# Third chunk's decays by scans from the open banks, key masks ahead of exponentials, early fades on GpSimd

## The chip, the cores and the metric

The kernel runs on one core of a Trainium2 chip. The metric is the time of one execution on the device, in microseconds (us). The kernel before takes 615.42 us, the median of three runs (615.21 to 615.60).

## What is computed

A state-space layer is followed by a weighted mixture of four small networks. Sequences of 768 tokens (4 of them, 8 heads of 32 channels, 16 states) go through the first in chunks. The decay from token j to token i is the exponential of a difference of summed logarithms, which is also the product of the decays in between:

```python
log_a = np.log(np.clip(a, 1e-06, 1.0))
...
    cum = np.cumsum(la, axis=-1)
    L = np.exp(cum[:, :, :, None] - cum[:, :, None, :])
    L = L * causal
    CB = np.einsum('bhin,bhjn->bhij', Cc, Bc)
    M = CB * L
    y_intra = np.einsum('bhij,bhjd->bhid', M, xc)
    y_inter = np.einsum('bhin,bhnd->bhid', Cc, state) * decay_to_i[:, :, :, None]
...
    state = decay_full[:, :, None, None] * state + np.sum(Bx, axis=2)
```

Its output is turned into 3072 tokens of 256 features, and each token gets the sum over four experts:

```python
p = domain_probs / (domain_probs.sum(-1, keepdims=True) + 1e-09)
for e in range(E):
    h = np.maximum(x @ w1[e], 0.0)
    out += p[:, e:e + 1] * (h @ w2[e])
```

Everything is float32.

## The kernel before

**Tiling.** Tokens come in 24 chunks of 128, numbered so that chunks 0 to 3 are the first of each of the four sequences, 4 to 7 the second, and so on. Four blocks of three pairs of chunks go through the experts one after the other. Expert weights come in pieces of 256 hidden features; sums of pieces (fast matrix multiplication with fewer products) are made on VectorE or GpSimd (`difference`, recorded at L1077), and from the second block on read back from DRAM. The products of the experts all have one line, L1017; the copies, sums and gates around them are L1026, L1031, L1044, L1052, L1175 and L1317.

**One chunk of the state-space part** needs four things. `mask` (L495, ScalarE) makes the key mask `ctm`: the chunk's C, once with the odd and once with the even heads set to zero. `score` (L502, TensorE) multiplies it with B into four PSUM banks of two chunks each. The decays L lie in `MT` or `LT`, and VectorE multiplies scores into them (L685 in the opening; L931 for one chunk at a time, L940 for two). A `fade`, recorded at L885 or L545, scales B by the decay to the chunk's end and puts it beside them. `inner` (L551, TensorE) makes outputs and the chunk's own state. From chunk 4 on, L963 adds what the earlier state gives; it reads `cts` (L915, GpSimd), which is the key mask scaled by decays.

**Decays are made in two ways.** Most chunks take exponentials: `sum_logs` turns logarithms of all decays into running sums by matrix products, the sums are stored to DRAM (`cum_d`), `load_decays` (L463) reads one chunk's back, spread over all partitions (`ab`, 512 KB), and `decay` (L526, ScalarE) makes eight exponentials. A causal cut then sets the upper half to zero, on VectorE (L532) where `CUT` says so and on GpSimd (L536) elsewhere. The chunks in `SCANS`, and chunks 0 and 1, take scans instead: `scan` (L519, VectorE) runs along a row of raw decays, multiplies by the decay and adds the identity, so that each partition's product starts at its own token, and no cut is wanted. For chunks 0 and 1 `spread` (L663) puts the raw decays on all partitions by a matrix product into banks, and the scan reads these; chunk 4 reads raw decays from DRAM (`acut_d`).

**The order.** The opening, up to L795, is written out by hand: instructions run in the order of the code on each engine. Behind it, `Plan` takes the rest: every piece of work is added with a duration for each engine that may do it, TensorE's order is given (`line`), and `Plan.run` simulates all engines, starting from the times given in `begin`, and picks on each engine the ready piece with the earliest due time. The order that comes out is then issued. `now` is the planner's clock at the end of the opening; `plan.taken` tells it which buffers are in use and from when their data can be had. A GpSimd piece that shares a port with VectorE is made to wait for the last VectorE instruction with two operands that stands ahead of it in the planned order (L1607).

**DMAs** of the loads and stores are issued by SP, in order. A load whose data is not yet stored holds up SP and all loads behind it.

Just behind the opening, TensorE's order is: second halves of two first-layer products (L726), two more first-layer products, the scores of chunks 2 and 3, four second-layer products (which need the first two second-layer pieces, `W[4]` and `W[5]`), the outputs of chunks 2 and 3, three more products, the scores of chunks 4 and 5, and so on:

```python
for seq, _ in plain[:EARLY]:
    line.extend(seq)
scores([2, 3])
...
line.extend(own_[:OWN])
outputs([2, 3])
```

Of the kernel before, what the change touches and what calls it, by code (L numbers as in the profile page):

```python
# [35 lines left out]
SCORED, OWN, LEAD, LEFT = 7, 4, 5, 3  # L36
SCANS = 4,
FILLED, EARLY, FADE = 3, 4, "DVE"
CUT = {(c, 0): "DVE" for c in range(2, 6)}
HORIZON, OPENING, LOADED = 26.0, 80.0, -0.5  # L40
ORDERS = (0, 1, 2, 3), (3, 1, 2, 0), (0, 1, 2, 3), (3, 1, 2, 0)
PAIRS_AT = ((1, 18, "s0"), (2, 1, "o0"), (2, 1, "s1"), (2, 24, "s2"), (3, 1, "o12")), (
    (1, 1, "s0"), (1, 24, "s1"), (2, 1, "o01"), (2, 24, "s2"), (3, 1, "o2"))
# [27 lines left out]
class Plan:  # L71
# [109 lines left out]
    def run(self, line, at, begin):  # L181
# [16 lines left out]
        stuck = 0  # L198
        self.stall, self.port, self.bus = [], 0.0, begin["SP"] + 4
        self.lanes = [begin["SP"] + .5 * i for i in range(LANES)]  # L200
# [160 lines left out]
def kernel(  # L361
# [25 lines left out]
    HALF = P // 2  # L387
    SPREAD = 2
    blocks = []
# [166 lines left out]
    def keep_state(c, A, y):  # L556
# [8 lines left out]
    aq0 = homes["V"][-1][:, 0].rearrange("p (t s) -> p t s", t=NT)  # L565
    aq1 = homes["V"][-2][:, 0].rearrange("p (t s) -> p t s", t=NT)
    a_q = [aq0, aq1]

# [10 lines left out]
    nc.scalar.dma_start(  # L579
        out=aq1.rearrange("(q r) t s -> q r (t s)", q=NQ)[:, 0], in_=a_rows[:, 1])  # L580
    nc.scalar.preload_act_table_set("natural_log_exp_and_others")
# [45 lines left out]
    nc.vector.reciprocal(total_p, total_p)  # L627
    clip(nc.vector, aq1.rearrange("p t s -> p (t s)"), own)
    nc.vector.memset(aq1[:, :, 0:1], 0.0)

# [28 lines left out]

    def spread(c, banks, half=0):  # L660
        for q, b in enumerate(banks):
            k = slice(32 * q, 32 * q + 32)
            nc.tensor.matmul(  # L663
                out=b[:, NT * P * half:NT * P * (half + 1)], lhsT=one[k].to_broadcast([32, P]),
                rhs=a_q[c][k].rearrange("p t s -> p (t s)"),
                start=True, stop=True, tile_position=(32 * q, 0))
# [89 lines left out]
    for fb in range(2, 4):  # L756
        load_w1(fb, homes["W"][fb])
    for fb in range(2):
        load_w2(fb, homes["W"][4 + fb])
    for c in range(2, 4):  # L760
        load_decays(c, homes["ab"][c - 2])
    for fb in range(2, 4):
        load_w2(fb, homes["W"][4 + fb])
# [4 lines left out]
    fade(0, MT[0], xb[0], LT[0])  # L768
    idle(four[2], 3)
    score([1], ctm[1:], xb[1:2], four, (2, 3, 1, 0))  # L770
    scan_quarters(LT[1], seven, 1, 0)
# [8 lines left out]
    for fb in range(2):  # L780
        first_half(seven[2 + fb], homes["W"][fb], yT0, 0)
    mask(2, ctm[0], xb[2])
    fade(1, MT[1], xb[1], LT[1])
# [17 lines left out]
    B512, B256 = {"DVE": D512, "POOL": 1.3}, {"DVE": D256, "POOL": .72}  # L801
    now = 12.5

# [28 lines left out]
    for c, i in ((2, 2), (3, 3)):  # L832
        st[c]["xb"] = plan.taken("xb", i, now)
    st[2]["ctm"] = plan.taken("ctm", 0, now)
    halves = [plan.taken("bank", homes["bank"].index(seven[2 + fb])) for fb in range(2)]
    for b in seven[:2]:
        plan.homes["bank"][homes["bank"].index(b)].free = now + .6
    for c in range(2, 4):
        st[c]["ab"] = plan.taken("ab", c - 2, now - 2.0 + 1.5 * c)
    for c in range(2):  # L840
        st[c]["A"] = plan.taken("A", c, now)
    g0 = gates[0, 0] = plan.taken("gate", 0, now)
    LTv = [plan.taken("V", 2 * (c % 2) + i, now) for c in SCANS for i in range(2)]
    neg = plan.taken("neg", 0, now - 3.0)
    cd, pd, ad = (plan.taken("dram", i, now) for i in range(3))

    def fetch(c):
        s = st[c]
        if "xb" not in s:
            s["xb"] = value("xb")  # L850
            dma(lambda e: load_tokens(c, s["xb"].t), 2 * len(turned(c)) - 1, 320,
                part=[s["xb"]])
        if c >= NSEQ:
            s["ah"] = value("ah")
            dma(lambda e: load_heads(c, s["ah"].t), len(turned(c)), 64,
                part=[s["ah"]], reads=[cd])
        if "ab" not in s:
            s["ab"] = value("ab")
            URGENT[len(plan.all)] = SOON if c < 6 else 0.0
            dma(lambda e: load_decays(c, s["ab"].t), 1, 512, part=[s["ab"]],  # L860
                reads=[ad if c in SCANS else cd])

    def decays(c):
# [6 lines left out]
        made, early = {}, c < blocks[0].n  # L870
        for h in range(0, NH, NQ) if c in SCANS else ():
            made[h] = dve(1.15, lambda e, h=h: scan(
                LT0[:, j], s["ab"].t[:, h * P:h * P + NQ * P], place(c, h) * P),
# [465 lines left out]
    def plain_first(fb):  # L1339
        w, y = weights["S", fb, 1], yT[0, 0]  # L1340
        if fb < len(halves):
            b = halves[fb]
            seq = [plan.add({"PE": .44}, lambda e: first_half(b.t, w.t, y.t, 1), reads=[w, y], writes=[b])]
            return seq, gated(b, gate_of(0, fb), 0)
# [111 lines left out]
    for fb in range(4):  # L1456
        loaded[fb, 1] = plan.taken("W", fb, now + (0.0 if fb < 2 else .5))
        loaded[fb, 2] = plan.taken("W", 4 + fb, now + (0.0 if fb < 2 else 1.5 + .75 * fb))
    for (fb, l), v in loaded.items():
# [135 lines left out]
    for i, w in enumerate(leave_last(len(blocks) - 1, O, LAST)):  # L1595
        behind.insert(len(behind) - TAILS[i], w)
    line.extend(behind)

    done = plan.run(line, now, {"PE": now, "DVE": now - 1.2, "ACT": now + .7, "POOL": now - 1.8,
                                "SP": now + LOADED})  # L1600
# [55 lines left out]
```

## Time and profile before

| what | us |
|---|---|
| median of three runs | 615.42 |
| the profiled execution, its own time | 614.88 |
| its span, first to last instruction | 613.2 |
| TensorE (PE) busy | 602.8 |
| VectorE (DVE) busy | 488.9 |
| ScalarE (ACT) busy | 299.2 |
| GpSimd (POOL) busy | 155.6 |

The profile is of one execution; times in it count from its first instruction. PE is TensorE's products, PEld its weight loads, which overlap them; PEq, ACTq and SPq are the engines' sequencers. A row of the timeline gives start and length in us, engine, line, operation, tiles (written <- read), shape and count; what stands in brackets is the engine's idle time before it and what ended it. Ends of matrix products are modelled, so that a stretch of products is better measured from its first start to the start of what follows. A row of the waits gives who waited for what: us in total, how often, and the longest.

Other rows of the opening that are used later (start, length, engine, what):

```profile
4.78 2.43 DVE L519 TENSOR_TENSOR_SCAN LT<-bank,ident 128x256 f32<-128x256 f32 x4 [0.39 <-PE bank L663]
5.39 0.94 SPq L460 DMA_DIRECT2D xb<-in_xbc_dram  x2
7.78 2.42 DVE L519 TENSOR_TENSOR_SCAN LT<-bank,ident 128x256 f32<-128x256 f32 x4
9.25 0.80 PE L502 MATMUL bank<-ctm,xb 32*128 32x256 f32 x8
9.98 0.70 PE L551 MATMUL bank<-MT,xb 128*32 128x144 f32 x16
10.49 0.98 SPq L483 DMA_DIRECT2D w<-in_w_dram  x2
11.86 0.82 SPq L463 DMA_DIRECT2D ab<-cum_d  x2
13.67 0.51 ACT L793 COPY v<-bank 128x128 f32<-128x128 f32 x2 [1.35 <-PE bank L551]
14.96 0.21 DVE L994 STREAM_TRANSPOSE S<-A 128x32 f32<-128x32 f32 x1 [3.50 <-ACT A L561]
```

### The profile page before, as it was taken

To read this page: it belongs to the slowest core of one execution; us is meant where nothing else is said; L and a number is where in the kernel's file an instruction comes from. 1 tells how busy PE (TensorE), PEld (TensorE's weight loads), DVE (VectorE), ACT (ScalarE), POOL (GpSimd) and SP (SyncE) were. 2 spreads that over 40 slices of the span, in tenths; PEclk is the share of its full clock that TensorE was granted. 3 is DMA by queue.
4 is the path that set the end of the run, shared out by engine and by line. 5 is a ranking of instruction groups with operands and counts; after the bars stand their busy time and mean duration, and the time that the engine had idled before them with its cause. 6 is when DMAs were issued, how large, how long until landed. Compare 5 with 4: busy or idle time off the path is not lost.

```text
span 613.2 us, 10055 instructions
## 1 busy us (share of the span) xinstructions
PE 602.8 (98%) x3377; PEld 513.5 (84%) x3377; DVE 488.9 (80%) x845; ACT 299.2 (49%) x707; POOL 155.6 (25%) x196
## 2 busy tenths in 40 slices
PE   8899999999999999999999999999999999999996
PEld 5677878888888888888888888888888888888885
DVE  5789898989999895877988988396785989575784
ACT  5766555389442327958252333834444142434441
POOL 5645654647443000777200100200000000000000
PEclk9999999999999999999999999999999999999999
DMA  7956668887733329792422325952242332964001
GB/s 224 318 160 211 218 207 279 291 290 259 271 105 100 84 43 359 257 294 107 154 88 79 115 43 151 317 194 91 70 137 66 106 73 40 356 202 130 1 0 53
DMA packets 88688, 100.30 MB, mean 164 GB/s; under 512 B 26932, under 2 KB 54204, under 8 KB 88636
## 3 DMA queue, kind: packets, MB, share of 16 engines
q1 hardware_dynamic: 88484, 99.60, 51.0%
q8 instruction: 27, 0.44, 0.3%
q14 instruction: 25, 0.20, 0.1%
q10 hardware_dynamic: 152, 0.05, 0.0%
HBM read 79.45 MB, written 20.17 MB: 162 GB/s over the span
## 4 chain that ended last, share of the span: by engine, by line
PE 91%; DVE 3%; DMA 2%; ACT 2%; POOL 1%; issue 1%; SPq 0%; DVEq 0%; ACTq 0%
PE bank L1017 87%; PE bank L551 2%; PE bank L502 2%; DMA ab<-cum_d 1%; DVE v L1044 1%; DVE v L1052 1%; PE bank L963 1%; ACT A L561 1%; ACT MT L526 1%; DVE bank L1175 1%; DMA cum_d<-cum 0%; DMA pr<-in_probs_dram 0%; POOL w L1077 0%; ACT v L978 0%; DVE v L1368 0%
## 5 line engine op out<-in xcount | busy, mean ns | idle before, releaser
L1017 PE MATMUL bank<-v,w 128*128 128x256 f32 x1592 | 377.7, 380 | 0.7 <-DVE v L1052 0.3
L1017 PEld LDWEIGHTS bank<-v,w 128*128 128x128 f32 x1592 | 301.0, 190 | 45.8 <-issue 3.3
L1017 PE MATMUL bank<-Y,w 128*128 128x256 f32 x692 | 177.5, 381 | 0.8 <-ACT LT L978 0.4
L1017 PEld LDWEIGHTS bank<-Y,w 128*128 128x128 f32 x692 | 130.2, 190 | 22.2 <-issue 1.5
L1317 ACT COPY v<-bank 128x512 f32<-128x512 f32 x109 | 63.9, 586 | 173.1 <-PE bank L1017 170.8
L1044 DVE TENSOR_TENSOR v<-v,v 128x512 f32<-128x512 f32 x185 | 136.1, 751 | 2.4 <-ACT v L1026 0.9
L1052 DVE SCALAR_TENSOR_TENSOR v<-bank,gate 128x512 f32<-128x512 f32 x144 | 98.8, 688 | 34.4 <-PE bank L1017 31.1
L1077 POOL TENSOR_TENSOR w<-w,w 128x512 f32<-128x512 f32 (+1 forms) x74 | 82.0, 1118 | 48.5 <-DVE v L1044 12.5
L1175 DVE TENSOR_TENSOR bank<-bank,v 128x512 f32<-128x512 f32 x85 | 58.1, 696 | 34.0 <-PE bank L1017 22.9
L1026 ACT COPY v<-bank 128x512 f32<-128x512 f32 x101 | 59.0, 587 | 51.3 <-PE bank L1017 40.2
L1031 ACT COPY bank<-v 128x512 f32<-128x512 f32 (+1 forms) x127 | 73.5, 590 | 11.5 <-DVE v L1052 6.0
L1017 PE MATMUL bank<-LT,w 128*128 128x256 f32 x276 | 69.8, 379 | 0.0
L1017 PEld LDWEIGHTS bank<-LT,w 128*128 128x128 f32 x276 | 52.4, 190 | 7.1
L526 ACT ACTIVATE MT<-ab,neg 128x128 f32<-128x128 f32 x168 | 53.2, 391 | 6.5 <-DMA ab<-cum_d 6.3
L536 POOL TENSOR_SCALAR_AFFINE_SELECT MT<-MT 128x512 f32<-128x512 f32 x39 | 26.9, 693 | 80.5 <-ACT MT L526 57.5
L940 DVE TENSOR_TENSOR MT<-bank,MT 128x512 f32<-128x512 f32 x40 | 25.3, 682 | 1.6 <-PE bank L502 1.4
L1044 DVE TENSOR_TENSOR v<-bank,v 128x512 f32<-128x512 f32 x27 | 18.6, 688 | 9.0 <-PE bank L1017 7.5
L1368 DVE TENSOR_TENSOR v<-v,v 128x256 f32<-128x256 f32 x55 | 21.4, 423 | 1.1 <-ACT v L1317 0.7
L1317 ACT COPY LT<-bank 128x512 f32<-128x512 f32 x12 | 7.0, 586 | 28.0 <-PE bank L1017 25.2
L1052 DVE SCALAR_TENSOR_TENSOR v<-v,gate 128x512 f32<-128x512 f32 x27 | 20.3, 753 | 0.4
L1052 DVE SCALAR_TENSOR_TENSOR LT<-bank,gate 128x512 f32<-128x512 f32 x18 | 12.4, 688 | 9.4 <-PE bank L1017 7.8
L502 PE MATMUL bank<-ctm,xb 32*128 32x256 f32 x192 | 14.4, 404 | 2.1 <-ACT ctm L495 2.1
(125 smaller groups left out, 306.4 us busy)
## 6 DMA issues: line engine op xcount, KB each, us to landing
w<-w_d SPq DMA_DIRECT2D x128, 256.0 KB
w<-in_w_dram SPq DMA_DIRECT2D x72, 256.0 KB
w_d<-w SPq DMA_DIRECT2D x64, 256.0 KB
ab<-cum_d SPq DMA_DIRECT2D x21, 512.0 KB
gate<-p_d SPq DMA_DIRECT2D x15, 384.0 KB
xb<-in_xbc_dram SPq DMA_DIRECT2D x17, 192.0 KB
xb<-in_xbc_dram SPq DMA_DIRECT2D x7, 320.0 KB
out_dram<-v SPq DMA_DIRECT2D x128, 16.0 KB
```

The costliest lines, as they stand in the source:

```text
L502: nc.tensor.matmul(out=views[r][:, j], lhsT=xb[j][k, OBT:OBT + P], rhs=ctm[j][k].rearrange("p t s -> p (t s)"), start=(j == 0), stop=True, ...
L526: nc.scalar.activation(out=MT[:, place(c, h), 0:P], in_=ab[:, h * P:h * P + P], func=AF.Exp, bias=neg[:, h % NT, NQ * real(c) + h // NT:NQ ...
L536: nc.gpsimd.affine_select(out=MT[:, h:h + n, 0:P], in_=MT[:, h:h + n, 0:P], compare_op=ALU.is_ge, fill=0.0, base=0, pattern=[[0, n], [1, P ...
L940: nc.vector.tensor_mul(to, g, to)
L1017: nc.tensor.matmul(out=o, lhsT=w[:, j], rhs=x if half is None else x[:, j], start=(start and j == 0), stop=(j == 1), skip_group_check=True)
L1026: act(.5, lambda e: nc.scalar.copy(out=flat(v), in_=bank.t), reads=[bank], writes=[v])
L1031: act(.54 if to - lo > FB else .32, lambda e: nc.scalar.copy(out=bank.t[:, lo:to], in_=flat(v)[:, lo:to]), reads=[v], writes=[bank])
L1044: plan.add(engines, lambda e: (on(e).tensor_add if sign > 0 else on(e).tensor_sub)(flat(v), whole(x), whole(y)), reads=[x, y], writes=[v], ...
L1052: dve(D512, lambda e: nc.vector.scalar_tensor_tensor(out=h.t, in0=whole(x).rearrange("p (j m) -> p j m", j=JJ), scalar=0.0, in1=g.t[:, 2 * ...
L1077: (on(e).tensor_add if sign > 0 else on(e).tensor_sub)(out, x, y)
L1175: dve(D512, lambda e: (nc.vector.tensor_add if sign > 0 else nc.vector.tensor_sub)(to.t, bank.t, whole(x)), reads=[x, bank], writes=[to])
L1317: act(.5, lambda e: nc.scalar.copy(out=flat(v), in_=bank.t), reads=[bank], writes=[v], hold=HOLD)
```

## The change

Chunk 2 (the third) joins the chunks that scan, and does it as chunks 0 and 1 do: its raw decays are loaded with chunk 1's (`a_q` has three parts), clipped with them, spread by four more matrix products into the free halves of the four banks that hold chunk 0's, ahead of chunk 1's scores, and scanned from there by VectorE in the planned part. Its exponentials, its causal cut and its load of stored sums go away. Its score products, and chunk 3's, are made one chunk at a time (L931) instead of two at once (L940).

The key masks of chunks 2 and 3 are both made in the opening, in buffers of their own; before, only chunk 2's was, and chunk 3's stood in the planned part.

The fades of chunks 2 to 5 go from VectorE to GpSimd (`FADE`).

SP issues chunk 3's stored sums first and all four second-layer pieces behind them; before, two of these stood ahead of the sums of chunks 2 and 3.

The planner's numbers change with it: its clock at the end of the opening, the starts of the engines, the time at which loads land, the duration of the second halves (1.02 instead of 0.44), and the place of one pair's scores (behind 20 products instead of 18).

```diff
-SCANS = 4,
-FILLED, EARLY, FADE = 3, 4, "DVE"
+SCANS = 2, 4
+FILLED, EARLY, FADE = 3, 4, "POOL"
-HORIZON, OPENING, LOADED = 26.0, 80.0, -0.5
+HORIZON, OPENING, LOADED = 26.0, 80.0, 0.0
-PAIRS_AT = ((1, 18, "s0"), (2, 1, "o0"), (2, 1, "s1"), (2, 24, "s2"), (3, 1, "o12")), (
+PAIRS_AT = ((1, 20, "s0"), (2, 1, "o0"), (2, 1, "s1"), (2, 24, "s2"), (3, 1, "o12")), (
...
-        self.stall, self.port, self.bus = [], 0.0, begin["SP"] + 4
+        self.stall, self.port, self.bus = [], 0.0, begin["SP"] + 3
...
-    SPREAD = 2
+    SPREAD = 3
...
-    aq1 = homes["V"][-2][:, 0].rearrange("p (t s) -> p t s", t=NT)
-    a_q = [aq0, aq1]
+    aq1 = homes["V"][-2].rearrange("p c (t s) -> p c t s", t=NT)
+    a_q = [aq0, aq1[:, 0], aq1[:, 1]]
...
-        out=aq1.rearrange("(q r) t s -> q r (t s)", q=NQ)[:, 0], in_=a_rows[:, 1])
+        out=aq1.rearrange("(q r) c t s -> q r c (t s)", q=NQ)[:, 0], in_=a_rows[:, 1:SPREAD])
...
-    clip(nc.vector, aq1.rearrange("p t s -> p (t s)"), own)
-    nc.vector.memset(aq1[:, :, 0:1], 0.0)
+    clip(nc.vector, aq1.rearrange("p c t s -> p (c t s)"), own)
+    nc.vector.memset(aq1[:, :, :, 0:1], 0.0)
...
-    for fb in range(2):
-        load_w2(fb, homes["W"][4 + fb])
-    for c in range(2, 4):
-        load_decays(c, homes["ab"][c - 2])
-    for fb in range(2, 4):
+    load_decays(3, homes["ab"][0])
+    for fb in range(4):
         load_w2(fb, homes["W"][4 + fb])
...
     idle(four[2], 3)
+    spread(2, four, 1, (2, 3, 1, 0))
     score([1], ctm[1:], xb[1:2], four, (2, 3, 1, 0))
...
-    mask(2, ctm[0], xb[2])
+    for c in range(2, 4):
+        mask(c, ctm[c], xb[c])
...
-    now = 12.5
+    now = 14.0
...
-    st[2]["ctm"] = plan.taken("ctm", 0, now)
+        st[c]["ctm"] = plan.taken("ctm", c, now)
+    st[2]["a"] = [plan.taken("bank", homes["bank"].index(b), now - 2.7) for b in four]
...
-    for c in range(2, 4):
-        st[c]["ab"] = plan.taken("ab", c - 2, now - 2.0 + 1.5 * c)
+    st[3]["ab"] = plan.taken("ab", 0, now + 1.5)
...
-    LTv = [plan.taken("V", 2 * (c % 2) + i, now) for c in SCANS for i in range(2)]
+    LTv = [plan.taken("V", i, now - 2.7) for i in range(2)]
...
         for h in range(0, NH, NQ) if c in SCANS else ():
+            if c < SPREAD:
+                made[h] = dve(1.2, lambda e, h=h: scan_quarters(
+                    LT0[:, j], [b.t for b in s["a"]], 1 - j, h // NQ),
+                    reads=s["a"][h // 2:h // 2 + 2], part=[LTv[h // NQ]])
+                continue
...
-            seq = [plan.add({"PE": .44}, lambda e: first_half(b.t, w.t, y.t, 1), reads=[w, y], writes=[b])]
+            seq = [plan.add({"PE": 1.02}, lambda e: first_half(b.t, w.t, y.t, 1), reads=[w, y], writes=[b])]
...
-        loaded[fb, 2] = plan.taken("W", 4 + fb, now + (0.0 if fb < 2 else 1.5 + .75 * fb))
+        loaded[fb, 2] = plan.taken("W", 4 + fb, now + 1.5 + .75 * fb)
...
-    done = plan.run(line, now, {"PE": now, "DVE": now - 1.2, "ACT": now + .7, "POOL": now - 1.8,
+    done = plan.run(line, now, {"PE": now, "DVE": now - 2.6, "ACT": now + .9, "POOL": now - 1.6,
                                 "SP": now + LOADED})
```

## The prediction

> **What bounds the kernel now.** I read the page first, then the busy time by stretches, then TensorE's waits, then the chain of waits and the timeline of the opening. The page and two of the stretches:
>
> ```profile
> PE 602.8 (98%) x3377; PEld 513.5 (84%) x3377; DVE 488.9 (80%) x845; ACT 299.2 (49%) x707; POOL 155.6 (25%) x196
> 20.00:25.00 5.00, 2.91 (x22) 2.21 (x19) 4.42 (x9) 4.85 (x17) 2.46 (x4) 1.00 1.03 349
> 300.00:400.00 100.00, 100.00 (x570) 86.27 (x572) 78.91 (x143) 43.81 (x96) 6.85 (x9) 1.00 0.43 132
> ```
>
> The columns of a stretch are its length, then PE, PEld, DVE, ACT and POOL, then the granted clock, the DMA share and GB/s. TensorE is busy for all of 300 to 400 at clock 1.00, and for 2.91 of 5 us from 20 to 25. So time can be won where TensorE stands idle, which is in the opening, and lost anywhere. TensorE's waits, longest first:
>
> ```profile
> PE bank L502 <- ACT ctm L495: 2.1, 1, 2.1
> PE bank L688 <- PEq L1648: 0.8, 1, 0.8
> PE bank L1433 <- DVE v L1368: 0.7, 1, 0.7
> PE bank L1017 <- ACT LT L978: 0.4, 1, 0.4
> ```
>
> The longest is one stop of 2.1 us: the scores of chunk 3 (L502) wait for its key mask (L495, on ScalarE). The chain of waits shows why that mask is late (start, length, what):
>
> ```profile
> 9.10 2.69 DMA cum_d<-cum
> ...
> 12.25 7.99 DMA ab<-cum_d
> ...
> 20.32 1.28 ACT MT L526 x4
> 21.60 0.58 ACT ctm L495 x2
> 22.18 1.01 ACT MT L526 x4
> ```
>
> The mask hangs on nothing late. It stands in ScalarE's queue behind exponentials that wait for decays out of DRAM. The timeline has the same place on the engines (start, length, engine, line, operation):
>
> ```profile
> 11.63 0.69 ACT L495 ACTIVATE ctm<-xb,tmask 128x128 f32<-128x128 f32 x2
> 18.90 2.70 ACT L526 ACTIVATE MT<-ab,neg 128x128 f32<-128x128 f32 x8 [3.97 <-DMA ab<-cum_d]
> 19.43 0.71 PE L502 MATMUL bank<-ctm,xb 32*128 32x256 f32 x8
> 22.23 0.71 PE L502 MATMUL bank<-ctm,xb 32*128 32x256 f32 x8 [2.09 <-ACT ctm L495]
> 22.88 3.72 PE L1017 MATMUL bank<-v,w 128*128 128x256 f32 x16
> 26.53 1.73 PE L551 MATMUL bank<-MT,xb 128*32 128x144 f32 x32
> 30.98 1.15 PE L502 MATMUL bank<-ctm,xb 32*128 32x256 f32 x16
> 32.05 3.80 PE L1017 MATMUL bank<-v,w 128*128 128x256 f32 x16
> ```
>
> **Part 1, the key mask of chunk 3 goes ahead of the exponentials.** Before, from the first score matmul (19.43) to the next product (22.88) are 3.45 us. The same sixteen score matmuls without a stop, for chunks 4 and 5, take from 30.98 to 32.05, which is 1.07. If both masks are there, TensorE gains 3.45 - 1.07 = 2.38 us. The mask needs chunk 3's tokens; their load is issued at 5.39 to 5.90, and the store issued behind it at 9.10 on the same queue has landed by 11.79. The added mask costs ScalarE 0.69 at about 12.3, inside the 1.35 us that it stands idle before the copies at 13.67. Were the tokens late, L793 would be late by as much, and TensorE with it. I take -2.38 (bounds: -2.38 to 0).
>
> **Part 2, chunk 2's decays by four scans from the open banks.** TensorE gets four more spread matmuls (eight passes) ahead of chunk 1's scores. Eight score passes of the same shape start at 9.25 and the next group at 9.98, so 0.73 with a change of operand; sixteen passes of chunks 4 and 5 take 1.07, so 0.54 for eight. Everything in this stretch of TensorE stands back to back, so I take +0.55 (bounds: 0, if the step hides in the 0.55 us of load idle ahead of 9.25, to +0.75). The clip of chunk 1's decays, now with chunk 2's beside them, goes from 256 to 512 columns, 0.25 us more (the row for 256) ahead of the first scan at 4.78, where VectorE stood idle 0.39: nothing; the longer memset stands where VectorE waits for the first load.
>
> The four scans take 2.42 us (the four scans from banks at 7.78). VectorE has 1.44 busy of 5 us from 10 to 15 and 1.88 from 15 to 20, and stands idle 3.50 us ahead of 14.96 for chunk 1's state, so they cost nothing. If that cover were gone, the gates of the first products would be late by up to 2.4 us, and they are wanted only at 22.88. The scans hold four banks until about 14.5, or 17.6 if they queue behind chunk 1's state; the next scores want them at about 20.
>
> Eight exponentials (2.70 us of ScalarE), one half-chunk causal cut on VectorE (0.69), one on GpSimd (0.63 to 0.72) and one load of 512 KB go away. SP now issues chunk 3's decays ahead of all four second-layer loads. That load still waits for the store landing at 11.79, and the four loads stand behind it in SP's queue: the first two were issued at 10.49 and 11.00 and now come after about 12.2. By size, chunk 3's decays have 1 MB less ahead of them: landing 20.24 goes to about 17 (1 MB at the 285 to 310 GB/s of these stretches is 3.4 us). The first two second-layer blocks land near 18 and 19, and are wanted at 21. Chunk 3's exponentials then run from 17 to about 19.7.
>
> **Part 3, fades on GpSimd.** Eight fades leave VectorE (six at 0.30 and two at 0.21 on average, so 2.2 us) and go to GpSimd, where the same shape takes 0.29. GpSimd's busy time from 20 to 35 is 2.46 + 4.66 + 3.76 = 10.9 of 15 us; four of the eight fall there, the first four mostly earlier. Each has to wait for VectorE's last two-operand instruction in the planned order, and the cuts, weight sums and state scales behind it wait with it. I count nothing on the path (bounds: -0.5 to +3; the rivals price the upper end).
>
> Fades and VectorE do hold each other up: VectorE's fade takes 213 ns at least and 746 at most, the long one beside a GpSimd cut that ran 1.55 us where others ran 0.63. The score products that the fades now run beside read a bank and one tile (0.41 to 0.42 in L685 and L931, in company of GpSimd or not), so I count no loss for them; rival (a) has the other case.
>
> **Part 4, the outputs of chunks 2 and 3.** TensorE reaches them at 26.53 + 0.55 - 2.38 = 24.7. Their last operands: scores end at about 21.0, and eight products of 256 columns instead of four of 512 take 8 x 0.41 = 3.3 us (L685, L931), against 4 x 0.69 = 2.7. They end at about 24.1 if the cuts and fades of chunk 3 (exponentials to 19.7, cut 0.7, fade 0.3) are done by 20.7. Before, from 26.53 to the next product at 28.19 took 1.66, while chunks 4 and 5 took from 36.38 to 37.49, 1.11. So between -0.55 and, with one gate of 0.69 in between, +0.7; I take -0.3.
>
> **Part 5, the new calibration.** The planner's start of 14.0 and its 1.02 for the first halves move the whole order, and one pair's scores go two products later. From 40 to 66 TensorE waits 1.6 us in all for VectorE and ScalarE; later it waits 0.4 for L978 and 0.9 in the tail. VectorE has about 2 us less to do by 33, and the weights are free to land 1.7 us earlier. Against that, another order may make other short waits. I take 0 (bounds: -1.0 to +2.0).
>
> **The sum:** -2.38 + 0.55 - 0.3 = -2.1 us. Against the profiled execution, 614.88 with a span of 613.2 and 1.7 around it, this is 612.8. That execution lies 0.54 below the median of 615.42, so the median comes to 613.3.
>
> **The rivals.** (a) The fades hold VectorE up. If each of the eight stops a VectorE sum for its whole 0.29 us, that is 2.3 us, and VectorE is the next bound: from 50 to 60 it is busy 10.00 of 10 us, and the chain runs through it from 46 to 63. The gain of 2.1 is then gone: 615.6 at the worst, 615.0 if two in three of them do. For it speaks the row of 746 ns above; against it that VectorE stood waiting for TensorE at 42.12 (1.19 us), so by then it had caught up. The Trainium skill, "SBUF — State Buffer", section "Who interferes with whom", has a rule for this: a VectorE instruction with two SBUF inputs and a GpSimd instruction that reads SBUF contend for one port pair, and the later one is blocked outright. The trace agrees as far as that one row goes; by the rule the sum would come to about no change, by the other rows it stays at -2.1.
>
> (b) Slower: GpSimd becomes the bound. The scaled queries of chunks 4 and 5 (L915, 1.41 us) ran from 32.09 to 33.5, after a wait of 1.24 for VectorE's fade. TensorE wanted them at 35.79 (L963), and wants them at about 33.7 after the change. Four fades ahead of them, each 0.29 and a wait of 0.5 to 0.8 for its turn (GpSimd's waits for VectorE here are 0.3 to 1.2), push them back by 3.2 to 4.4 us, the cut that went gives 0.7 back: done at 36.0 to 37.2. By the upper end the outputs of chunks 4 and 5 start at 37.3 instead of 35.8, and all behind them 1.5 late: 616.9. It decides once the scaled queries come over 2.2 us later than now. Against it: GpSimd's weight sums can go to VectorE, which the planner decides by due times.
>
> (c) The masks do not come ahead in fact: chunk 3's tokens land after 13.6. ScalarE then stands before L793, and the 0.55 is paid besides: 616.0. Against it speaks the landing at 11.79 above.
>
> **How the numbers follow.** What a measurement of this kernel can tell from no change is about 0.2%, here 1.23 us. The forecast has a chance of 0.56 (its own range 611.8 to 614.2), (a) 0.15, (b) 0.23, (c) 0.06. Faster by over 0.2%: the forecast, 0.56. Slower by over 0.2%, that is over 616.65: nearly all of (b) and a little of (c), 0.24. Between: 0.20. The range runs from 611.8, where the calibration gives another 1.5 us, to 617.2, where GpSimd's lateness is carried on; that leaves out about 0.1 at each end.
>
> **What would show it.** In the profile after: no wait of L502 for L495; ScalarE's second mask before 14 us; sixteen score matmuls of chunks 2 and 3 in one go at about 20; four scans from banks between 11 and 18; the outputs of chunks 2 and 3 starting at 24.5 to 25; L963 at about 33.7 without a wait for GpSimd. The prediction is wrong if a wait of over 1 us stands at one of the last two, or if the waits from 40 to 130 add up to over 1 us more than now.

## The result, and the profile after

The changed kernel takes 611.65 us (median of 6, 610.93 to 612.22) against 615.32 us (median of 6, 614.11 to 617.87): ratio 0.9938, interval 0.9917 to 0.9959. A second series gave 611.32 against 615.78, ratio 0.9937 (0.9917 to 0.9957). The forecast was 613.3, with a range from 611.8. The sign and the place were right, the forecast gain was too small.

In the new listing the lines of the planned part that are used here are 4 later: L1017 is L1021, L931 is L935, L963 is L967, L1077 is L1081. The page, two stretches (length, then PE, PEld, DVE, ACT, POOL, clock, DMA share, GB/s) and TensorE's waits after the change:

```profile
PE 603.0 (99%) x3385; PEld 514.7 (84%) x3385; DVE 488.3 (80%) x843; ACT 296.6 (49%) x699; POOL 153.9 (25%) x204
20.00:25.00 5.00, 5.00 (x41) 3.92 (x44) 3.59 (x10) 1.90 (x7) 4.92 (x9) 1.00 0.92 289
300.00:400.00 100.00, 100.00 (x578) 86.02 (x578) 78.86 (x142) 43.79 (x96) 7.41 (x10) 1.00 0.42 130
PE bank L688 <- PEq L1652: 0.8, 1, 0.8
PE bank L1437 <- DVE v L1372: 0.7, 1, 0.7
PE bank L688 <- DVE LT L519: 0.5, 1, 0.5
PE bank L1021 <- ACT LT L982: 0.4, 1, 0.4
PE bank L502 <- ACT A L561: 0.4, 1, 0.4
```

TensorE is busy for all of 20 to 25, and the stop of 2.1 us is gone. The last row shown is new. Rows of the chain of waits and of the timeline of the opening, in the same columns as before:

```profile
9.25 3.35 DMA cum_d<-cum
...
12.66 4.16 DMA ab<-cum_d
```

```profile
11.56 2.42 DVE L519 TENSOR_TENSOR_SCAN LT<-bank,ident 128x256 f32<-128x256 f32 x4
12.20 1.28 ACT L495 ACTIVATE ctm<-xb,tmask 128x128 f32<-128x128 f32 x4
16.91 2.45 ACT L526 ACTIVATE MT<-ab,neg 128x128 f32<-128x128 f32 x8 [1.38 <-DMA ab<-cum_d]
20.03 1.15 PE L502 MATMUL bank<-ctm,xb 32*128 32x256 f32 x16
21.11 3.72 PE L1021 MATMUL bank<-v,w 128*128 128x256 f32 x16
24.76 1.19 PE L551 MATMUL bank<-MT,xb 128*32 128x144 f32 x32
25.88 2.86 PE L1021 MATMUL bank<-v,w 128*128 128x256 f32 x12
27.50 0.31 ACT L917 ACTIVATE dec<-ah 128x128 f32<-128x128 f32 x1 [0.32 <-DMA ah<-cum_d]
27.71 0.63 ACT L982 COPY v<-bank 128x256 f32<-128x256 f32 x2
28.37 1.50 ACT L561 COPY A<-bank 32x32 f32<-32x32 f32 x8
29.16 1.90 PE L502 MATMUL bank<-ctm,xb 32*128 32x256 f32 x16 [0.42 <-ACT A L561]
30.99 3.80 PE L1021 MATMUL bank<-v,w 128*128 128x256 f32 x16
```

Both masks stand at 12.20, the scans run from banks at 11.56, chunk 3's exponentials start at 16.91, and sixteen score matmuls run in one go at 20.03. At 29.16 TensorE comes to the scores of chunks 4 and 5 too early. They want banks that ScalarE still empties (L561), and ScalarE was held up by a decay (L917) that waited for a DMA behind the late store (3.35 us instead of 2.69). In the second profile of the changed kernel the loads came earlier, and the stop is hardly there:

```profile
26.07 2.86 PE L1021 MATMUL bank<-v,w 128*128 128x256 f32 x12
...
28.86 1.22 PE L502 MATMUL bank<-ctm,xb 32*128 32x256 f32 x16
...
30.00 2.29 PE L1021 MATMUL bank<-v,w 128*128 128x256 f32 x9
```

The starts of the same TensorE groups, read off the timelines, in us (difference to before in brackets):

| group | before | after | after, second profile |
|---|---|---|---|
| second halves, L726 | 13.99 | 14.60 (+0.61) | 14.79 (+0.80) |
| scores of chunks 2 and 3 | 19.43 | 20.03 (+0.60) | 20.22 (+0.79) |
| product behind them | 22.88 | 21.11 (-1.77) | 21.30 (-1.58) |
| product behind outputs of 2 and 3 | 28.19 | 25.88 (-2.31) | 26.07 (-2.12) |
| product behind scores of 4 and 5 | 32.05 | 30.99 (-1.06) | 30.00 (-2.05) |
| product behind outputs of 4 and 5 | 37.49 | 36.43 (-1.06) | 35.44 (-2.05) |
| product behind the scores at 80 to 83 | 84.37 | 82.06 (-2.31) | 81.16 (-3.21) |
| last but one turn of the output | 604.17 | 601.85 (-2.32) | 600.95 (-3.22) |

From 84 us on nothing moves any more. But 2.3 to 3.2 us in the profiles stand against 3.7 to 4.5 in the medians: one more thing differs between executions.

### The profile page after: what moved, and what is told of

Read it like the earlier page. It is cut to its first block, busy times and chain, and to the rows that moved or that the text cites. A ratio compares the mean times of both kernels' runs of the same rounds, so it can differ in the third digit from the quotient of the medians.

```text
span 610.5 us, 10066 instructions
## 1 busy us (share of the span) xinstructions
PE 603.0 (99%) x3385; PEld 514.7 (84%) x3385; DVE 488.3 (80%) x843; ACT 296.6 (49%) x699; POOL 153.9 (25%) x204
## 4 chain that ended last, share of the span: by engine, by line
PE 93%; DMA 2%; ACT 2%; DVE 1%; issue 0%; POOL 0%; SPq 0%; ACTq 0%; DVEq 0%; POOLq 0%
PE bank L1021 88%; PE bank L502 2%; PE bank L551 2%; DMA ah<-cum_d 1%; ACT A L561 1%; PE bank L967 1%; DMA ab<-cum_d 1%; PE bank L688 1%; DMA cum_d<-cum 1%; POOL w L1081 0%; ACT v L982 0%; DVE bank L1179 0%; ACT MT L526 0%; DVE LT L519 0%; DVE v L1372 0%
## 5 line engine op out<-in xcount | busy, mean ns | idle before, releaser
L1021 PE MATMUL bank<-v,w 128*128 128x256 f32 x1640 | 385.3, 380 | 0.0
L1021 PEld LDWEIGHTS bank<-v,w 128*128 128x128 f32 x1640 | 310.4, 190 | 45.3 <-issue 2.1
L1021 PE MATMUL bank<-Y,w 128*128 128x256 f32 x692 | 177.5, 381 | 0.8 <-ACT LT L982 0.4
L1021 PEld LDWEIGHTS bank<-Y,w 128*128 128x128 f32 x692 | 130.2, 190 | 22.2 <-issue 1.5
L1321 ACT COPY v<-bank 128x512 f32<-128x512 f32 x106 | 62.1, 585 | 173.9 <-PE bank L1021 172.9
L1048 DVE TENSOR_TENSOR v<-v,v 128x512 f32<-128x512 f32 x174 | 130.2, 760 | 1.3
L1081 POOL TENSOR_TENSOR w<-w,w 128x512 f32<-128x512 f32 (+1 forms) x74 | 80.2, 1094 | 55.1 <-DVE v L1048 15.1
L1030 ACT COPY v<-bank 128x512 f32<-128x512 f32 x99 | 57.9, 586 | 49.2 <-PE bank L1021 42.7
L1179 DVE TENSOR_TENSOR bank<-bank,v 128x512 f32<-128x512 f32 x79 | 53.7, 694 | 33.4 <-PE bank L1021 23.7
L1035 ACT COPY bank<-v 128x512 f32<-128x512 f32 x126 | 72.8, 594 | 10.6 <-DVE v L1056 7.3
L1021 PE MATMUL bank<-LT,w 128*128 128x256 f32 x228 | 58.0, 379 | 0.0
L1021 PEld LDWEIGHTS bank<-LT,w 128*128 128x128 f32 x228 | 43.2, 190 | 6.1 <-issue 0.3
L1372 DVE TENSOR_TENSOR v<-v,v 128x256 f32<-128x256 f32 x45 | 17.8, 417 | 1.1 <-ACT v L1321 0.7
L1048 DVE TENSOR_TENSOR v<-v,LT 128x512 f32<-128x512 f32 x25 | 16.9, 683 | 0.3
```

The source lines that it names most:

```text
L1021: nc.tensor.matmul(out=o, lhsT=w[:, j], rhs=x if half is None else x[:, j], start=(start and j == 0), stop=(j == 1), skip_group_check=True)
L1030: act(.5, lambda e: nc.scalar.copy(out=flat(v), in_=bank.t), reads=[bank], writes=[v])
L1035: act(.54 if to - lo > FB else .32, lambda e: nc.scalar.copy(out=bank.t[:, lo:to], in_=flat(v)[:, lo:to]), reads=[v], writes=[bank])
L1048: plan.add(engines, lambda e: (on(e).tensor_add if sign > 0 else on(e).tensor_sub)(flat(v), whole(x), whole(y)), reads=[x, y], writes=[v], ...
L1081: (on(e).tensor_add if sign > 0 else on(e).tensor_sub)(out, x, y)
L1179: dve(D512, lambda e: (nc.vector.tensor_add if sign > 0 else nc.vector.tensor_sub)(to.t, bank.t, whole(x)), reads=[x, bank], writes=[to])
```

## The experiments

Where the text gives short waits between products, it is the time from one start to the next beyond the usual 0.217 us, summed over a stretch wherever it is more than 0.12 us. By this count the kernel before has 1.65 us from 36 to 66 and 0.28 from 66 to 130, and the changed kernel has 0.40 and 0.28 in both of its profiles.

**Chunk 3's mask alone.** From the kernel before:

```diff
     mask(2, ctm[0], xb[2])
+    mask(3, ctm[1], xb[3])
...
     st[2]["ctm"] = plan.taken("ctm", 0, now)
+    st[3]["ctm"] = plan.taken("ctm", 1, now)
```

> The kernel before, with chunk 3's key mask made in the opening and nothing else changed. My prediction's term, taken by itself: the stop of 2.1 us at the scores goes and TensorE gains 2.38 us for good (613.0 against 615.4). Rival: the stop hides a second one. Chunk 3's decays still land at 20.2 us, so its exponentials end at about 23.9 instead of 24.5 and its products at about 26.3 instead of 26.9; TensorE then waits at the outputs of chunks 2 and 3 (L551), which start at about 26.0 instead of 26.5. Gain 0.5 us (614.9).

614.58 us, ratio 0.9990 (0.9970 to 1.0009). TensorE's timeline and waits, and the store of the running sums from the chain of waits:

```profile
9.20 3.56 DMA cum_d<-cum
...
19.52 1.15 PE L502 MATMUL bank<-ctm,xb 32*128 32x256 f32 x16
20.60 3.72 PE L1019 MATMUL bank<-v,w 128*128 128x256 f32 x16
25.29 0.40 PE L551 MATMUL bank<-MT,xb 128*32 128x144 f32 x2 [0.97 <-ACT MT L526]
25.88 0.41 PE L551 MATMUL bank<-MT,xb 128*32 128x144 f32 x2 [0.19 <-DVE MT L942]
27.74 1.17 PE L551 MATMUL bank<-MT,xb 128*32 128x144 f32 x28 [1.45 <-POOL w L1079]
28.85 2.86 PE L1019 MATMUL bank<-v,w 128*128 128x256 f32 x12
```

The scores lose their stop, and 22.88 becomes 20.60. The outputs then wait three times, 2.6 us in all, and the next product comes at 28.85 instead of 28.19. (The releaser of the last wait is GpSimd by this view; the weight sum named has nothing to do with the outputs, and VectorE's last score product, behind the late exponentials, ended just before.) The second stop of the rival is there. Its size in this profile is partly chance: the store took 3.56 us, 0.87 more than in the profile of the kernel before, and the exponentials behind it began at 19.96 instead of 18.90. At 615.17 us this execution is also the slowest of the six with a mean granted clock of 0.999 or more; their median is 613.48, against 614.4 for such executions of the kernel before (table below). So by itself the mask gives about 1 us of its 2.38, and over all executions no gain that is clear of the noise. In five of its twelve executions the clock is 0.997 or less, although no single stop of the profile is longer than 1.45 us: the three waits lie close together, 2.6 us within 3.4.

**Everything but the scan.** The kernel before with mask, fades, calibration, and both loads of decays ahead of the four second-layer pieces:

```diff
-    for fb in range(2):
-        load_w2(fb, homes["W"][4 + fb])
     for c in range(2, 4):
         load_decays(c, homes["ab"][c - 2])
-    for fb in range(2, 4):
+    for fb in range(4):
```

> Everything of the change but the scan: chunk 2 keeps its exponentials and its load, both loads of decays stand ahead of the four second-layer pieces, the mask is in the opening, fades are on GpSimd, calibration is the new one. My sum: without the spread TensorE is 0.55 us earlier, and everything else stays; 0.5 us faster than the changed kernel. Rival: chunk 3's decays land at about 19 us instead of 16.9, and ScalarE makes sixteen exponentials instead of eight, to about 22.5; products end at about 25, TensorE comes to the outputs at 24.2 and waits 0.8 us or more, so that the scan pays for its spread: the same as the changed kernel, or up to 1 us slower.

613.68 us, ratio 0.9966 (0.9952 to 0.9979), some 2 us slower than the changed kernel. (The profiled execution, 614.73, is one of the slower ones.)

```profile
19.41 1.15 PE L502 MATMUL bank<-ctm,xb 32*128 32x256 f32 x16
22.09 3.69 PE L1017 MATMUL bank<-v,w 128*128 128x256 f32 x16 [1.54 <-DMA w<-in_w_dram]
25.71 0.65 PE L551 MATMUL bank<-MT,xb 128*32 128x144 f32 x4
27.38 1.17 PE L551 MATMUL bank<-MT,xb 128*32 128x144 f32 x28 [1.01 <-POOL w L1077]
```

Two loads of decays ahead of the weights make the weights late, 1.54 us at 22.09, and sixteen exponentials still make the outputs late, 1.01 us at 27.38. So my sum, in which the scan was a cost of 0.55 and no gain, is wrong. The scan is what lets both the mask and the order of the loads pay: it takes eight exponentials off ScalarE and 512 KB off the queue ahead of the weights.

**Fades back on VectorE** in the changed kernel (`FADE = 3, 4, "DVE"`).

> The changed kernel with the fades of chunks 2 to 5 back on VectorE. After the change TensorE's waits for VectorE and ScalarE between 40 and 66 us came to 0.5 us instead of 1.6. Theory A: that is VectorE's relief of 2.2 us by the fades; here the waits come back to 1.3 to 1.6 us and the kernel is 1 us slower than the changed one. Rival B: it is the new order that the calibration gives; here the waits stay at about 0.5 us and the time within 0.3 us of the changed one. Rival C: fades on GpSimd cost more than they save in the turn-taking; here it is faster than the changed kernel by 0.5 us or more.

612.27 us, ratio 0.9944 (0.9929 to 0.9958), against 0.9938 and 0.9937 with the fades on GpSimd. In this profile the decays were issued at 11.57, about as early as in the second profile of the changed kernel (11.81), so it is compared with that one. Both come to the product behind the outputs of chunks 2 and 3 at 26.07. Here the product behind the scores of chunks 4 and 5 starts at 30.43 instead of 30.00, and the short waits from 36 to 66 are 0.93 us instead of 0.40; the last but one turn of the output starts at 601.83 instead of 600.95. So in the changed kernel the fades' place is worth 0.9 us in the profile and 0.6 to 1.0 in the median. That is nearest to theory A in the time; the short waits come back in part.

**The old calibration** in the changed kernel:

```diff
-    now = 14.0
+    now = 12.5
...
-    done = plan.run(line, now, {"PE": now, "DVE": now - 2.6, "ACT": now + .9, "POOL": now - 1.6,
+    done = plan.run(line, now, {"PE": now, "DVE": now - 1.2, "ACT": now + .7, "POOL": now - 1.8,
```

(and the four smaller numbers of the diff.)

> The changed kernel with the old calibration: the planner's clock 12.5, the old starts of the engines, 0.44 for the second halves, the pair's scores behind 18 products. Theory A (fades): the gain stays, within 0.4 us of the changed kernel, and the waits between 40 and 66 us stay below 0.8. Rival B (calibration): those waits are 1.3 us or more, and the kernel is 1 us slower than the changed one. For the new stop of 1.2 us at the scores of chunks 4 and 5 (TensorE waits for ScalarE's state copies, which stand behind two key masks and a decay that waits for a DMA): with the old clock the copies may come ahead of the decay, and the stop would then be at most 0.5.

613.35 us, ratio 0.9963 (0.9949 to 0.9978), 1.7 to 2.0 slower than the changed kernel. The stop at the scores of chunks 4 and 5 is nearly gone (28.64 to 29.84), but the store landed early in this profile, 2.22 us after its issue, so that this does not show what the order does for it. The short waits come to 1.2 us from 36 to 66 and 0.8 from 66 to 130 (0.40 and 0.28 in the changed kernel). From the product behind the outputs of chunks 4 and 5 to the last but one turn of the output it is 567.10 us here, 566.68 in the kernel before, and 565.42 and 565.51 in the changed kernel. B is nearer in size, though the waits do not stand where B had them.

**Scan and masks, with neither fades nor calibration**, that is both of the last two edits at once.

> The changed kernel without two of its parts: the fades are on VectorE and the calibration is the old one; scan, masks and order of the loads stay. Theory: scan and masks together carry the gain, the stop at the scores and the clock with it; the opening is as in the changed kernel to 25.9 us, and what the old calibration costs behind it (0.8 us in the profile, 1.7 in the median with fades on GpSimd) is the difference: 613.0 to 613.5. Rival: without both the order falls back to the waits of before between 40 and 66 us (1.6 us); 614 or more.

612.93 us, ratio 0.9958 (0.9943 to 0.9972), just below the range expected. The opening is the same to 25.8 us, and the short waits from 36 to 66 are 1.4 us. Scan, masks and the order of the loads carry about two thirds of the gain; fades and calibration bring the rest, together.

**Fades alone, and calibration alone**, in the kernel before.

> The kernel before with its early fades on GpSimd and nothing else. From putting them back on VectorE in the changed kernel (same end of TensorE in the profile) I expect nothing here either: within 0.6 us of before, the stop of 2.1 us at the scores still there, waits between 40 and 66 us of 1.2 to 1.7. Rival: the fades relieve VectorE only where the calibration is the old one; then these waits fall below 0.8 and the kernel is 0.8 us faster.

616.66 us, ratio 1.0021 (1.0007 to 1.0035): slower.

> The kernel before with the new calibration alone. Taking it out of the changed kernel cost 0.8 us in the profile (new stops at 39, 88 and 104 us). Theory: the waits between 40 and 66 us were 1.3 to 1.7 in both kernels that had the old fades and no scan, and 0.4 to 0.9 in all with the new calibration or the scan; so here they fall below 0.9, and the kernel is 0.6 to 1 us faster than before, with the stop at the scores still there. Rival: calibration only fits the opening that it was measured on; without the scan the order is no better, and the kernel is within 0.4 us of before or slower.

619.05 us, ratio 1.0056 (1.0035 to 1.0078): slower by over 3 us. Both have a new stop for VectorE's sums near 59 us:

```profile
PE bank L1017 <- DVE v L1044: 1.9, 1, 1.9
```

is the row of the calibration alone (1.2 with the fades alone). The calibration that helps the changed kernel hurts this one: it fits the opening that it belongs to. This profile also shows something else, in its stretches:

```profile
19.80:23.20 3.40, 1.36 (x17) 0.62 (x14) 2.81 (x4) 3.11 (x11) 1.41 (x2) 1.00 1.05 405
23.20:26.60 3.40, 3.40 (x9) 2.72 (x9) 3.30 (x8) 3.40 (x13) 2.42 (x4) 0.50 0.76 228
57.40:60.80 3.40, 1.49 (x7) 1.01 (x7) 3.40 (x7) 0.82 (x3) 1.12 (x2) 1.00 0.93 292
60.80:64.20 3.40, 3.40 (x10) 2.65 (x9) 1.98 (x3) 1.16 (x3) 1.37 (x3) 0.50 0.90 301
```

The column ahead of the DMA share is the granted clock. Behind each stretch in which TensorE stood for about 2 us, the clock is one half for 3.4 us, which costs 1.7. The sixteen products at 22.93 take 5.3 us to the outputs there, and 3.65 in the kernel before. The executions of the kernel before fall apart in the same way, by their mean granted clock over the span (62 executions, the three series of before that ran beside the experiments):

```
clock            executions   us: least   median   most
0.999 and more       22         613.7      614.4    615.3
0.996 to 0.997       35         615.1      616.0    617.2
0.994                 5         617.1      617.8    618.0
```

One stretch of 3.4 us at one half is 0.003 of the span's mean. All 12 executions of the changed kernel have 0.999 or more.

The traces also show why a stop of the same length halves the clock in one execution and not in another. In every profile the changes of the granted clock stand whole multiples of 3.41 us apart; in this one they are at 23.23, 26.64, 60.77 and 64.19. On this grid, the windows ahead of the two halved stretches have 2.04 and 1.91 us in which TensorE stood. In the profile of the kernel before, the grid has a boundary at 21.00, which cuts the stop of 2.09 us into 0.86 and 1.23, and the clock stays at 1.00. In all thirteen profiles, every window with 1.91 us or more of standing is followed by one half, and none with 1.64 or less is. An estimate from these figures: a stop of 2.09 us that falls anywhere on a grid of 3.41 puts 1.64 us into one window in 65% of cases and 1.91 us in 49%; 40 of 62 executions are 65%.

**TensorE kept busy through the stop.** The kernel before, with products of ones into a spare bank between the two chunks' scores:

```diff
         for j, c in enumerate(cs):
+            if j and between is not None:
+                for _ in range(2):
+                    idle(between)
```

> The kernel before, with two matrix products of ones (four passes over 512 columns, about 1.7 us) into a spare bank between the scores of chunk 2 and of chunk 3, so that TensorE is busy while it would stand for the late key mask; the wait itself stays. Executions of the kernel before with a mean granted clock of 0.999 or more took 614.1 to 615.3 us, those at 0.997 took 615.1 to 616.9, those at 0.994 took 617.1 to 618.0. In the profile of the calibration alone the clock stands at one half for 3.41 us right behind each of its two stops of 2 us. Theory: a stop of about 2 us takes the clock down to one half in some executions, for 3.41 us, which is 1.7 us lost each time; here the clock is 0.999 or more in nearly all executions, the spread falls to about 1.5 us and the median by about 1 us (ratio 0.998), though the scores come no earlier. Rival: the lower clock is not caused by the stop at the scores; clocks and median stay as before (ratio 1.000).

614.47 us (613.99 to 615.72), ratio 0.9988 (0.9977 to 0.9999). All 12 executions have a clock of 0.998 or more; of the 22 of before beside them 15 have 0.997 or less.

```profile
19.68 0.71 PE L505 MATMUL bank<-ctm,xb 32*128 32x256 f32 x8
20.32 1.99 PE L691 MATMUL bank<-const-float32-1.0 128*128 128x512 f32 x4
22.45 0.71 PE L505 MATMUL bank<-ctm,xb 32*128 32x256 f32 x8
23.09 3.72 PE L1022 MATMUL bank<-v,w 128*128 128x256 f32 x16
```

The scores of chunk 3 start 2.77 us behind those of chunk 2 (2.80 before), so nothing is won on the way, and yet 1.1 us of the median goes. The theory of the clock holds. (This run's profile, at 0.998, has a clock of 1.00 from 6.63 to 610.79; what is missing from 1 lies in the last 2 us of the span.)

**Two tries to go further.** Chunk 3's state copies on VectorE, and the decays of chunks 4 and 5 behind the copies (edits in `outputs` and `decays`):

> The changed kernel, with the new stop at the scores of chunks 4 and 5 taken away: chunk 3's state copies go from ScalarE to VectorE, and the two decays of chunks 4 and 5 (exponentials that wait for a DMA) come behind the copies of chunks 2 and 3 on ScalarE. Theory: the banks come free by 28.6, the scores start without a stop, and the time is 1 us below the changed kernel in its slow executions and 0.3 in its fast ones; median 0.5 us lower. Rival: the gain is lost again to a wait within the next 30 us (the products that follow, or the scaled queries, which now wait for later decays).

611.98 us, ratio 0.9946 (0.9925 to 0.9966). The scores of chunks 4 and 5 start at 28.63 without a stop and the product behind them at 29.70, but from 36 to 66 the short waits rise from 0.40 to 1.8 us. The rival holds.

The scores at 80 us four products later (`(2, 5, "s1")`):

> The changed kernel with the scores of the pair behind the outputs at 79 us moved four products later. In both profiles of the changed kernel TensorE waits there for 0.73 us (at 81 to 82 us), as in the kernel before (84.4): the outputs hold two banks and the scores four, and the next product wants a bank that ScalarE still empties. Theory: with four products in between, the copies run beside them; the wait goes and the time falls by 0.7 us to 610.7. Rival: the order behind it changes and the wait comes back elsewhere before 130 us; the same time within 0.4 us.

612.45 us, ratio 0.9958 (0.9945 to 0.9971). The wait behind the scores goes, and another comes ahead of the fourth product behind them:

```profile
87.88 1.10 PE L1021 MATMUL bank<-v,w 128*128 128x256 f32 x4 [0.53 <-ACT bank L1035]
```

Neither beats the changed kernel. The repeat of the changed kernel, used throughout above:

> The changed kernel once more, for a second profile and a tighter ratio. In its first profile the store of the running sums took 3.35 us to land (2.69 before) and TensorE stopped 1.2 us at the scores of chunks 4 and 5; the run of that profile, 612.22, was the slowest of six. Theory: the stop hangs on when that store lands. In a profile where it lands within 2.7 us the stop is at most 0.4, the span is about 1 us shorter, and the ratio stays near 0.994. Rival: the stop is there whenever, by ScalarE's order alone, and the difference of the executions has another place.

Its stop at the scores was 0.07 us beyond the usual (28.86 to 30.00, against 1.07 without a wait), with the decays issued at 11.81 instead of 12.66, and its span 609.6 instead of 610.5. The profiled time, 611.32, is the series' median. The theory fits. A third profile of the same opening, that of the kernel with the later scores, has its decays issued at 11.88 and a stop of 0.44 us (28.70 to 30.21); three profiles are few.

## Why the forecast had the right sign and too small a size

**Part 1 (-2.38 forecast).** From the first score to the next product it is 1.08 us in both profiles after, against 3.45: -2.37. The size is exact, but the reason was half the story. I costed the mask as if it could be had by itself, and by itself it gives about 1 us. The outputs of the same chunks stood behind the same late load, and a stop followed there (experiment with the mask alone).

**Part 2 (+0.55).** Measured +0.60 and +0.80 at the scores. The scans ran at 11.56 in VectorE's idle time, at 2.42 us for four, as costed. The decays landed at 16.8 (forecast: about 17), the masks did not wait for tokens. What the sum missed is that the scan was needed for the rest of it.

**Part 3 (0, bounds -0.5 to +3).** With the new calibration, putting the fades back costs 0.9 us in the profile and 0.6 to 1.0 in the median, more than the 0.5 of the bound; with the old one, fades on GpSimd are no gain (613.35 us, against 612.93 without them). Rivals (a) and (b) did not happen: the scaled queries ran from 30.96 to 32.37, earlier than before, and TensorE's L967 did not wait for them. One moved fade took 1.07 us beside a scan, where others took about 0.3: so the two engines do hold each other up, and VectorE waited once for a fade, 0.69 us at 30.80, but TensorE came to the outputs of chunks 4 and 5 without a wait. The row of 746 ns was read with the wrong partner: that fade of VectorE began at 30.20, when the GpSimd cut of 1.55 us (from 28.61) had ended, and ran beside a GpSimd weight sum (30.13 to 30.85).

**Part 4 (-0.3).** From the outputs of chunks 2 and 3 to the next product it is 1.12 instead of 1.66 us: -0.54, the better end of the bounds. The eight score products were taken as 8 x 0.41 = 3.3 us; they start every 0.33 us and take 2.7 (21.25 to 23.98). Not foreseen was the next stop, 1.25 us in one profile and 0.07 in the other, as the store of the running sums landed late or not.

**Part 5 (0, bounds -1.0 to +2.0): the first mis-sized term.** Between 37 and 84 us TensorE gained 1.25 and 1.16 us, where the sum has nothing and the bound is 1.0. I argued that an order made anew could go either way and took the middle. The experiments say more: with the old calibration the changed kernel loses 1.7 to 2.0 us in the median, and the new one in the old opening loses 3, of which 1.7 is a second halved stretch of the clock. The start that the planner is told was 1.5 us ahead of the trace in the kernel before (12.5 against 13.99 for L726), and 14.0 against 14.60 in the changed one; that comparison could have been made from the profile of before.

**The term that was missing: the clock.** I made the sum against one execution of the kernel before, at a clock of 0.999, and carried its difference to the median. But about two thirds of the executions of before lose 1.7 us or more to a halved clock behind the stop at the scores, and none of the changed kernel's does. With full clocks the kernels stand at 614.4 and 611.4 (the medians of such executions, over several series), a gain of 3.0; the medians over all executions differ by 3.7 and 4.5. The Trainium skill, "TensorE: Matmul & The Clock Gate", Part 1, says that the clock is gated to one half or full by activity in free-running windows of 3413 ns. The trace agrees: the two stretches at one half are 3.41 us long each, and the grid begins at another time in each profile (the first record of the clock stands at 3.93 us in the kernel before, at 4.76 and 6.81 in the changed one). The Trainium skill, "TensorE: Matmul & The Clock Gate", "HAM oscillation", speaks of idle gaps over about 3.4 us; here gaps of 2.1 us were enough in 40 of 62 executions, and the measurement decides. That it is some executions and not all follows from where the grid cuts the stop, as the profiles show; what the unprofiled executions did is known by their mean clock alone.

**The step that failed** is the end of the sum, with Part 5 at nothing and the clock left out. The forecast of 613.3 stands 1.65 us above 611.65. Of this, 1.0 is the clock (615.42 that the forecast was carried to, against 614.4 at full clock), 0.9 is the gain at full clock (3.0 instead of 2.1, with the 1.2 us between 37 and 84 us as its largest term that the sum does not have), and the series stood 0.25 above the 611.4. The signs that were named (the masks, the scores in one go, the scans, the outputs at 24.76 and 24.95, L967 at 34.72 and 33.73 without a wait for GpSimd) all came; none of them asked about the clock.

With scan, masks and the order of the loads at 612.93, fades and calibration together account for the last 1.3 to 1.6 us. How they share it is not settled by these runs, and the scan was not run alone: each was tried with and without the other, and what one is worth depends on the other and on the opening.

## What to carry to other kernels

Before a wait is costed as a gain, ask what the same late data holds up next: a stop that is taken away alone can stand again, in part, a few instructions later, and an edit that looks like a cost (here the scan) can be what makes 2 us of the others' gain. A planner's starting times are measurements of one opening and have to be measured again when the opening changes; elsewhere the same numbers can cost 3 us. Look at the granted clock of every execution and not only of the profiled one: here a stop of 2.1 us on TensorE cost nearly 4 in most executions.

## What the runs showed of the hardware

A TensorE stop of about 2 us halved its clock for the next 3.41 us: seen twice in the profile of the calibration alone, and by the mean clock in 40 of 62 executions of the kernel before. Products of ones in the gap prevented it (12 of 12 executions at 0.998 or more). In these profiles it depended on how long TensorE stood within one window of a grid of 3.41 us: 1.91 us and more halved the clock, 1.64 and less did not. A single stop of about 1.5 us did it rarely: the kernel with everything but the scan stood 1.54 us at 22.09 and has a mean clock of 0.999 or more in 11 of 12 executions. Several short ones close together did it more often: with the mask alone, 5 of 12 executions have 0.997 or less.

The store of the running sums (96 KB) landed 2.22 to 3.56 us after its issue in profiles of kernels whose opening up to it is nearly the same (2.22, 2.65, 2.69, 3.03, 3.04, 3.10, 3.35, 3.56). As the loads of decays wait for it in SP's queue, all of the opening behind it moves by up to 1.3 us from one profile to the next.
